# A planner's keys and DMA rates: attention into a gated FFN on one core, batch 0's v products and first half reordered

## The chip, the cores and the metric

The kernel runs on one core of one Trainium2 chip. The metric is the device time of one execution in microseconds: for the kernel before, the median of 8 runs is 378.05 us (376.56 to 378.98). The profile comes from one further execution, which took 377.98 us.

A core has five engines with queues of their own. TensorE (PE in the profile, PEld its weight loads) multiplies, VectorE (DVE), ScalarE (ACT) and GpSimd (POOL) compute, and SyncE (SP) here only issues DMA transfers. GpSimd issues DMA transfers as well, those that change the type on the way among them. Each queue is worked off in its order; between queues, semaphores make one wait for another.

## The reference

Inputs: q, k and v of shape (8, 8, 576, 64) (batch, heads, sequence, head width), s of shape (8, 8, 576), and the weights of the FFN, all float32.

```python
scores = scale * np.matmul(q, k.transpose(0, 1, 3, 2))
cum = np.cumsum(np.maximum(s, 0.0), axis=-1)
bias = -(cum[:, :, :, None] - cum[:, :, None, :])
scores = np.where(causal, -1e9, scores + np.minimum(bias, 0.0))
attn = softmax(scores);  out = np.matmul(attn, v)
x = out.transpose(0, 2, 1, 3).reshape(4608, 512)
xn = x / np.sqrt(np.mean(x * x, axis=-1, keepdims=True) + 1e-6) * rms_g
g = xn @ w_gate;  val = xn @ w_val          # 512 -> 1536
return (g * sigmoid(g) * val) @ w_out       # 1536 -> 512
```

Because cum rises along the sequence, the factor exp(-(cum_i - cum_j)) splits into a factor of the query, which the division by the sum cancels, and a factor exp(cum_j) of the key. The kernel multiplies v by that factor (the tiles vw, whose 65th column holds the factor itself, so that one matmul gives the sum as well).

## The kernel before, in words

**Order of the work.** The kernel first describes all of its operations to a planner (`Plan`, line 76), in Python, before anything runs. Each operation has an engine, a time in us that the planner counts for it, a `key` (lower goes first) and the operations that it depends on by the tiles that it reads and writes; `R.after(o, p)` (line 132) adds a dependence. `schedule` (line 136) then plays a list schedule: at each step it takes the engine that can start earliest, and on it, of the operations that are ready, the one with the lowest key; VectorE, ScalarE and GpSimd hold back for an operation of lower key that becomes ready within half of the candidate's time (line 199). What comes out is only the order on each engine; it is written into the program once, and on the chip each queue keeps it whatever the real times are. PSUM has 8 banks; each use names a group and how many banks the group may hold at once (`room`, line 162); `small_bank` (line 390) is a group of at most two.

**DMA transfers in the planner.** All transfers share one line: `dma_free` (line 148) is when the last one planned ends. A transfer begins at the later of that and its issue plus `lags[0]`, takes `dma`, and its data count as there `lags[1]` later (lines 216 to 219). Transfers that GpSimd issues go through 8 lanes (line 190). A transfer on SP may not be issued more than 3.0 us ahead of the end of all planned traffic (line 192). Rates stand in the helpers: `load_runs` (line 399, batches 0 and 1 of q and k in runs, cast to bf16 by GpSimd's transfers), `load_rows` (line 405, five blocks of 128 sequence positions, the last of 64), `load_w` (line 416, halves of the weights).

**Attention.** A batch has 4 head pairs and two halves, 8 units (`unit_scores`, line 539, `unit_av`, line 568). A unit's scores are three or five pairs of matmuls with K in place as weights, two exponentials on ScalarE into a tile E, and masks on GpSimd; Ea to Ed are the units of the first half (query blocks 0 and 1, of key blocks 0 and 1), Ee to Eh those of the second half, which also need key blocks 2 to 4. Then AV, on VectorE a reciprocal (rZ) and a product into x_blk. After a half's four units come its RMS norm (`attention`, line 628): squares summed (`att_square`, on ScalarE, for one block of batch 0 on VectorE), alpha = (mean + 1e-6)^-0.5 on GpSimd (`att_alpha`, tile al), and `att_out`: scale on ScalarE, four transposes on TensorE and a product with g into xnT, for batches 0 to 2. For batches 3 to 7 the scale is on VectorE and a DMA transpose on SP writes xnT. The keys are `key + step * (u + 1.5)` for a unit's AV and k2 = `key + step * 5.5` for the first half's norm; for batch 0 key is -78 and step 3, so that k2 is -61.5, which is the key of unit 4's AV too.

**K and Q.** Batches 0 and 1 come as runs (tiles raw, laid over q_nat and k_nat: batch 0 over q_nat, batch 1 over k_nat) and are transposed on TensorE (`prep_transpose`, line 427). For batches 2 to 7, SP loads fp32 rows into k_nat and q_nat, VectorE casts a block to bf16 (k_bf, q_bf) and a DMA transpose on SP writes the block into KT or QT (`prep_cast`, line 440). ScalarE squares all of K and Q for a check of magnitude (`raw_norm`, line 456, for batches 0 and 1). Of the tile k_nat, block i is free for batch 2 only once the i-th square of batch 1 is done. v has one tile (v_nat), whose block is free for the next batch when its product (`prep_v`, line 464; VectorE for batch 0, GpSimd after it) is done; the q and k loads of batch 2 wait for all of batch 1's products (line 766).

**FFN.** Nine chunks of 512 tokens (line 741). Chunk c has 12 or 24 pairs of matmul groups (`ffn1_group`), with tanh on ScalarE and two products on VectorE into Hs, then four output blocks (`ffn2`) whose stores go through SP. Keys of chunk c start at 36c. Attention of batch c+1 has keys from 36c + 1, its casts and transposes 36c - 14, the loads of batch c+2 36c + 16 in the order k, q, v, and the stores 36c. So on SP, in a chunk, stores go first when ready, then the transposes of the next batch, then the loads of the one after.

The setup of batch 0 begins at line 692. Its lines for v and attention, 723 to 731, are in the diff below; wl[2:], the second halves of the gate and value weights, wait for the mask of unit 3, and the runs of batch 1 for the first mask of unit 7.

Of the kernel before, what the change touches and what calls it, by code (L numbers as in the profile page):

```python
# [75 lines left out]
class Plan:  # L76
# [59 lines left out]
    def schedule(self):  # L136
        ops = self.ops
        for o in ops:
            o.succ = []
        left = {}  # L140
        for o in ops:
            left[o.n] = len(o.preds)
            for p in o.preds:
                ops[p].succ.append(o)
        free = {}
        table = {}
        pool = {}
        self.dma_free = 0.0
        order = []
        held = [[0.0, None] for _ in self.banks]  # L150

        def ready(o):
            t = 0.0
            for p, raw in o.preds.items():
                q = ops[p]
                if q.eng == o.eng and not q.dma:
                    t = max(t, q.done if raw and o.eng != "pe" else q.start)
                else:
                    t = max(t, q.done + self.HOP)
            return t  # L160

        def room(o):
            group, cap, n = o.takes[0].group, o.takes[0].cap, len(o.takes)
            for t in sorted(f for f, _ in held if f is not None):
                free = sum(1 for f, _ in held if f is not None and f <= t)
                busy = sum(1 for f, g in held if g == group and (f is None or f > t))
                if free >= n and busy + n <= cap:
                    return t
            return None

        lanes = [0.0] * self.LANES

        def add(o):
            pool.setdefault(o.eng, []).append((ready(o), o))

        for o in ops:
            if not left[o.n]:
                add(o)
        while any(pool.values()):
            best = None  # L180
            for e, cand in pool.items():
                f = free.get(e, 0.8)
                can = []
                for r, o in cand:
                    if o.takes:
                        t = room(o)
                        if t is None:
                            continue
                        r = max(r, t)
                    if o.dma and e == "pool":  # L190
                        r = max(r, lanes[0] + self.HOP)
                    if o.dma and e == "sp":
                        r = max(r, self.dma_free - 3.0)
                    can.append((o.key, o.n, r, o))
                if not can:
                    continue
                t = max(f, min(x[2] for x in can))
                k = min((x for x in can if x[2] <= t + 0.02), key=lambda x: x[:2])
                if e in ("dve", "act", "pool"):
                    soon = [x for x in can if x[:2] < k[:2] and x[2] < t + self.AHEAD * k[3].us]  # L200
                    if soon:
                        k = min(soon, key=lambda x: x[2])
                s = max(f, k[2])
                if best is None or s < best[0]:
                    best = (s, e, k[3], f)
            s, e, o, f = best
            pool[e] = [(r, q) for r, q in pool[e] if q is not o]
            o.wait = s - f
            if o.kind is not None:
                if table.get(e) not in (None, o.kind):  # L210
                    s += self.TABLE
                table[e] = o.kind
            o.start = s
            free[e] = s + o.us
            o.done = s + o.us + o.lat
            if o.dma:
                begin = max(self.dma_free, s + o.us + o.lags[0])
                self.dma_free = begin + o.dma
                o.done = self.dma_free + o.lags[1]
                if e == "pool":  # L220
                    lanes[:] = lanes[1:] + [o.done]
            for bank in o.takes:
                i = min((i for i, (t, _) in enumerate(held) if t is not None),
                        key=lambda i: held[i][0])
                bank.phys = i
                held[i][:] = [None, bank.group]
            for bank in o.uses:
                bank.left -= 1
                if not bank.left:
                    held[bank.phys][0] = max(u.done for u in bank.users) + self.HOP  # L230
            order.append(o)
            for q in o.succ:
                left[q.n] -= 1
                if not left[q.n]:
                    add(q)
        assert len(order) == len(ops)
        self.order = order
        return order
# [7 lines left out]
def kernel(  # L246
# [104 lines left out]
    def I(eng, method, us, key=None, kind=None, dma=0.0, lags=(1.2, 1.2), **kw):  # L351
        outs = [kw[n] for n in ("out", "accum_out") if n in kw]
        ins = [a for n, a in kw.items()
               if n not in ("out", "accum_out") and isinstance(a, (bass.AP, View))]
        f = getattr(ENG[eng], method)
        o = R.add(eng, us, lambda: f(**{n: real(a) for n, a in kw.items()}), outs, ins, key=key,  # L356
                  lat=LAT[eng], kind=kind, dma=dma,
                  name=outs[0].bank.name if isinstance(outs[0], View) else outs[0].name)
        o.lags = lags
        return o  # L360
# [37 lines left out]

    def load_runs(b, which, h0, h1, key):
        p0 = KP * which  # L400
        return I("pool", "dma_start", 0.8, key=key, dma=(4.0, 3.45)[b] * (h1 - h0) / 8, lags=(0.9, 1.3),
                 out=raw[b][p0 : p0 + KP, h0:h1, :, :].rearrange("p h c d -> p h (c d)"),
                 in_=(k, q)[which][b, h0:h1, :, :].rearrange("h (p c) d -> p h (c d)", c=KC))

    def load_rows(dst, src, b, eng, key):
        ops = []
        for sc in range(NB):
            n = 128 if sc < 4 else 64
            ops.append(I(eng, "dma_start", 0.88 if eng == "pool" else 0.4, key=key,
                         dma=1.28 * n / 128,  # L410
                         lags=(1.2, 1.2 if b < 2 else 4.2),
                         out=dst[0:n, sc], in_=src[b, :, sc * 128 : sc * 128 + n, :].rearrange(
                             "h p d -> p h d")))
        return ops

    def load_w(which, lo, hi, key):
        if which == 2:
            return I("pool", "dma_start", 0.84, key=key, dma=9.6 * (hi - lo) / 12,
                     out=wout_sb[:, lo:hi, :],
                     in_=moe_w_out[lo * 128 : hi * 128, :].rearrange("(fc p) d -> p fc d", p=128))  # L420
        dst, src = ((wg_sb, moe_w_gate), (wv_sb, moe_w_val))[which]
        return I("pool", "dma_start", 0.76, key=key, dma=8.9 * (hi - lo) / DF,
                 out=dst[:, :, lo:hi],
                 in_=src[:, lo:hi].rearrange("(cc p) f -> p cc f", p=128))

# [202 lines left out]
    def attention(b, key, step, cap):  # L628
        Es = {}
        two = 2 if b >= NTWO else 1  # L630
        sc = [unit_scores(b, range(u, u + two), [key + step * i for i in range(u, u + two)], Es,
                          max(cap, 2 * two)) for u in range(0, 2 * HP, two)]
        norms = []
        if b == 0:
            for u in range(HP + 1, 2 * HP):
                R.after(sc[u], sc[HP - 1])
        for hf in range(2):
            for u in range(HP * hf, HP * hf + HP):
                norms.append(unit_av(b, u, key + step * (u + 1.5), Es))
            tbs = (0, 1) if hf == 0 else (2, 3, 4)  # L640
            k2 = key + step * (HP * hf + HP + 1.5)
            for tb in tbs:
                att_square(b, tb, k2, "dve" if b == 0 and tb == 1 else "act")
            att_alpha(b, tbs[0], tbs[-1] + 1, k2)
            for tb in tbs:
                att_out(b, tb, k2)
        return norms
# [72 lines left out]
    for hp in range(HP):  # L720
        prep_transpose(0, 0, hp, -80 + hp, "dve")
        prep_transpose(0, 1, hp, -80 + hp, "act")
    gp_ = small_bank()
    mms(0.1, [(gp_[:, 0:CC], g4, ident_F[0:CC, 0:CC], True, True, True)], key=-75)
    I("dve", "tensor_copy", 0.1, key=-75, out=g_sb, in_=gp_[:, 0:CC])
    prep_w(0, "act", -70)
    vops = [prep_v(0, sc, "dve", -70) for sc in range(NB)]
    norms = attention(0, -78, 3, 4)
    R.after(vops[2], norms[2])
    for o in wl[2:]:  # L730
        R.after(o, masks[0, HP - 1])
    raw_norm(0, 20)
# [213 lines left out]
```

## Time and profile before

| what | value |
|---|---|
| median of 8 runs | 378.05 us (376.56 to 378.98) |
| profiled execution, its own time | 377.98 us |
| its span, first to last instruction | 376.2 us |
| instructions | 7766 |
| TensorE busy | 344.5 us, 92% |
| VectorE / ScalarE / GpSimd busy | 252.8 / 230.6 / 129.1 us |
| first FFN matmul | 27.02 us |
| granted clock at 0.5 | 192.05 to 195.46 us, and the end |
| chain that ended last | PE 56%, DVE 13%, DMA 11%, SP queue 6%, ACT 5% |
| first scores of batches 2 to 7 | 85.65, 117.14, 149.74, 189.83, 231.48, 272.38 us |

How to read it. The timeline lists an engine's instructions by start and duration, with the idle time ahead of them and what ended it in brackets; adjacent instructions of one kind are merged (x3). Tiles are named out<-in. SPq and POOLq are queues: an SP entry is the issue of a transfer, and what it waited for counts into its duration; when the data land is told by the trace's landing record. The table of waits adds up such idle times by the pair of waiting and releasing line. All helper operations carry line 356 and matmuls 371 or 373, so groups are told apart by their tiles. The granted clock is TensorE's, as a share of full speed.

### The profile page before, as it was taken

What the parts mean: (1) busy time and instruction counts of PE and PEld (TensorE: products, weight loads), DVE (VectorE), ACT (ScalarE), POOL (GpSimd) and SP (SyncE); (2) the same over time, 40 slices, a digit from 0 to 9 for tenths busy, and PEclk for the clock granted to TensorE, in tenths of its full rate; (3) what the DMA queues carried; (4) which work ended last, traced back from release to release, by engine and by line L of the source; (5) the groups of instructions that cost most, each with busy time, mean ns of one, the idle gap of its engine ahead of it and who ended that gap; (6) DMA issues with size and microseconds to landing.
All of it is one profiled execution on the core that took longest, in us unless ns stands there. A gap on an engine that the chain in (4) does not pass through costs nothing.

```text
span 376.2 us, 7766 instructions
## 1 busy us (share of the span) xinstructions
PE 344.5 (92%) x2907; PEld 208.7 (55%) x2934; DVE 252.8 (67%) x486; ACT 230.6 (61%) x469; POOL 129.1 (34%) x211
## 2 busy tenths in 40 slices
PE   3769999999999999799979988988999999999993
PEld 3548876698667874687425443444445444444441
DVE  6575954886946896489928893869578737816830
ACT  3857699697788827765657646871887533313321
POOL 8887334332561436133703470244323110000000
PEclk9999999999999999999989999999999999999998
DMA  7999994977996996689767986599650140011002
GB/s 121 212 225 208 198 178 102 192 172 151 187 167 173 172 190 127 180 155 197 133 107 183 194 169 115 146 201 193 114 153 9 30 129 19 0 73 42 0 34 86
DMA packets 138356, 51.13 MB, mean 136 GB/s; under 512 B 127300, under 2 KB 132936, under 8 KB 138312
## 3 DMA queue, kind: packets, MB, share of 16 engines
q1 hardware_dynamic: 131688, 41.13, 54.7%
q0 software_dynamic: 6624, 9.44, 14.3%
q8 instruction: 25, 0.41, 0.5%
q14 instruction: 19, 0.16, 0.2%
HBM read 38.16 MB, written 9.44 MB: 127 GB/s over the span
## 4 chain that ended last, share of the span: by engine, by line
PE 56%; DVE 13%; DMA 11%; SPq 6%; ACT 5%; issue 4%; POOL 3%; DVEq 0%; ACTq 0%; POOLq 0%
PE psc L373 8%; PE psh L373 7%; PE psb L373 7%; PE psg L373 7%; PE psd L373 7%; PE psa L373 7%; PE pse L373 6%; SPq L356 6%; PE psf L373 6%; DMA q_nat<-in_q_dram 4%; DVE Hs L356 3%; ACT sq_scr L356 3%; DMA v_nata<-in_v_dram 2%; DVE x_blkb L356 2%; DMA out_dram<-osbc 2%
## 5 line engine op out<-in xcount | busy, mean ns | idle before, releaser
L373 PEld LDWEIGHTS <-wv_sb 128*128 128x128 bf16 x624 | 60.9, 99 | 38.7 <-issue 6.3
L373 PEld LDWEIGHTS <-wg_sb 128*128 128x128 bf16 x624 | 59.1, 99 | 33.3 <-issue 5.5
L373 PEld LDWEIGHTS <-Hs 128*128 128x128 bf16 x432 | 41.3, 98 | 50.4 <-DVE Hs L356 2.7
L356 POOL TENSOR_TENSOR vwb<-v_nata,wT 128x512 bf16<-128x512 f32 (+1 forms) x20 | 21.1, 1071 | 13.4 <-DMA v_nata<-in_v_dram 13.0
L356 POOL TENSOR_SCALAR_AFFINE_SELECT Ea<-Ea 128x512 bf16<-128x512 bf16 x8 | 5.2, 647 | 59.1 <-ACT Ea L356 59.1
L356 ACT ACTIVATE sq_scr<-x_blka 128x512 bf16<-128x512 bf16 x19 | 12.0, 631 | 15.8 <-DVE x_blka L356 15.5
L373 PE MATMUL psf<-xnT,wv_sb 128*128 128x256 bf16 (+1 forms) x116 | 20.6, 313 | 0.2
L356 DVE CAST k_bf<-k_nat 128x512 bf16<-128x512 f32 (+1 forms) x30 | 17.1, 581 | 5.3 <-DMA k_nat<-in_k_dram 5.3
L356 ACT ACTIVATE sq_scr<-x_blkb 128x512 bf16<-128x512 bf16 x20 | 12.6, 630 | 12.5 <-DVE x_blkb L356 12.0
L356 POOL TENSOR_TENSOR vwa<-v_nata,wT 128x512 bf16<-128x512 f32 (+1 forms) x15 | 16.7, 1129 | 7.9 <-DMA v_nata<-in_v_dram 7.9
L356 DVE CAST q_bf<-q_nat 128x512 bf16<-128x512 f32 (+1 forms) x30 | 17.5, 593 | 2.8 <-DMA q_nat<-in_q_dram 2.8
L373 PE MATMUL pse<-xnT,wg_sb 128*128 128x256 bf16 (+1 forms) x102 | 18.2, 314 | 0.1
L373 PE MATMUL psd<-xnT,wg_sb 128*128 128x256 bf16 (+1 forms) x95 | 18.1, 325 | 0.1
L373 PE MATMUL psc<-wout_sb,Hs 128*128 128x512 bf16 x69 | 17.0, 379 | 1.1 <-DVE Hs L356 0.9
L373 PE MATMUL psh<-wout_sb,Hs 128*128 128x512 bf16 x70 | 16.6, 379 | 0.9 <-DVE Hs L356 0.8
L373 PE MATMUL psc<-xnT,wg_sb 128*128 128x256 bf16 (+1 forms) x83 | 15.2, 321 | 1.8 <-DVE xnT L356 1.3
L373 PE MATMUL psg<-wout_sb,Hs 128*128 128x512 bf16 x70 | 16.6, 379 | 0.1
L356 ACT ACTIVATE sq_scr<-q_bf 128x1024 bf16<-128x1024 bf16 (+1 forms) x18 | 16.5, 916 | 0.2
L373 PE MATMUL psb<-xnT,wg_sb 128*128 128x256 bf16 (+1 forms) x95 | 16.3, 307 | 0.1
L356 ACT ACTIVATE sq_scr<-k_bf 128x1024 bf16<-128x1024 bf16 (+1 forms) x18 | 16.3, 908 | 0.0
L373 PE MATMUL psb<-xnT,wv_sb 128*128 128x256 bf16 (+1 forms) x84 | 15.3, 322 | 0.2 <-DVE u_sbc L356 0.2
L356 DVE SCALAR_TENSOR_TENSOR x_blkb<-x_blkb,alb,gB 128x512 bf16<-128x512 bf16 x15 | 12.4, 876 | 4.6 <-POOL alb L356 4.5
(456 smaller groups left out, 859.2 us busy)
## 6 DMA issues: line engine op xcount, KB each, us to landing
k_nat<-in_k_dram SPq DMA_DIRECT2D x24, 256.0 KB, 4.7
q_nat<-in_q_dram SPq DMA_DIRECT2D x24, 256.0 KB, 5.4
v_nata<-in_v_dram SPq DMA_DIRECT2D x24, 256.0 KB, 5.0
out_dram<-osba SPq DMA_DIRECT2D x12, 256.0 KB, 2.3
out_dram<-osbb SPq DMA_DIRECT2D x12, 256.0 KB, 2.3
out_dram<-osbc SPq DMA_DIRECT2D x12, 256.0 KB, 2.4
v_nata<-in_v_dram POOLq DMA_DIRECT2D x8, 256.0 KB, 10.4
wg_sb<-in_moe_w_gate_dram POOLq DMA_DIRECT2D x2, 768.0 KB, 12.2
```

Source lines behind the costliest of these rows:

```text
L356: o = R.add(eng, us, lambda: f(**{n: real(a) for n, a in kw.items()}), outs, ins, key=key, lat=LAT[eng], kind=kind, dma=dma, name=outs[0]. ...
L373: nc.tensor.matmul(out, lhsT=lhsT, rhs=rhs, start=st, stop=sp)
```

## The change

Seven places change; the set of operations and their data stay the same.

- In the planner, an SP transfer may be issued from 2.0 us ahead of the end of the last transfer of SP's own queue (`sp_free`), no longer 3.0 us ahead of the end of all traffic. The single line of traffic, dma_free, stays for when a transfer begins.
- The counted DMA times of `load_runs`, `load_rows` and `load_w` become smaller.
- The key k2 of batch 0's first half goes from -61.5 to -64.5; unit 5's mask has key -63, unit 6's -60, unit 7's -57.
- The transpose of g takes a bank of a group of its own.
- The v products of batch 0 keep the key -70 for key blocks 0 and 1 and get -62 for blocks 2 to 4; block 2's product is made to follow the normalisation of unit 3 (before: of unit 2), whose AV has the key -64.5.

```diff
         lanes = [0.0] * self.LANES
+        sp_free = 0.0
...
                     if o.dma and e == "sp":
-                        r = max(r, self.dma_free - 3.0)
+                        r = max(r, sp_free - 2.0)
...
                 o.done = self.dma_free + o.lags[1]
+                if e == "sp":
+                    sp_free = self.dma_free
...
-        return I("pool", "dma_start", 0.8, key=key, dma=(4.0, 3.45)[b] * (h1 - h0) / 8, lags=(0.9, 1.3),
+        return I("pool", "dma_start", 0.8, key=key, dma=(3.95, 3.35)[b] * (h1 - h0) / 8, lags=(0.9, 1.3),
...
-                         dma=1.28 * n / 128,
+                         dma=(1.08 if eng == "pool" else 1.2) * n / 128,
...
-            return I("pool", "dma_start", 0.84, key=key, dma=9.6 * (hi - lo) / 12,
+            return I("pool", "dma_start", 0.84, key=key, dma=8.0 * (hi - lo) / 12,
...
-        return I("pool", "dma_start", 0.76, key=key, dma=8.9 * (hi - lo) / DF,
+        return I("pool", "dma_start", 0.76, key=key, dma=7.8 * (hi - lo) / DF,
...
-            k2 = key + step * (HP * hf + HP + 1.5)
+            k2 = key + step * (HP * hf + HP + 1.5) - (3 if b == 0 and hf == 0 else 0)
...
-    gp_ = small_bank()
+    gp_ = bank("g", 1)
     mms(0.1, [(gp_[:, 0:CC], g4, ident_F[0:CC, 0:CC], True, True, True)], key=-75)
     I("dve", "tensor_copy", 0.1, key=-75, out=g_sb, in_=gp_[:, 0:CC])
     prep_w(0, "act", -70)
-    vops = [prep_v(0, sc, "dve", -70) for sc in range(NB)]
+    vops = [prep_v(0, sc, "dve", -70 if sc < 2 else -62) for sc in range(NB)]
     norms = attention(0, -78, 3, 4)
-    R.after(vops[2], norms[2])
+    R.after(vops[2], norms[3])
```

## The prediction

> **What bounds the kernel now.** First the page, for the shares of the engines: TensorE is busy 92% of the span, every other engine under 70%. The table by windows then says where TensorE is not busy: 11.1 us of the first 27.02 us, 1.5 us from there to 120 us, 12.8 us between 120 and 282 us, 6 us after that. So there are two places to win: the start, and the middle. The last 94 us hold TensorE work alone.
>
> The start, from the timeline (start, duration, engine, line, operation):
> ```profile
> 18.13 1.28 DVE L356 TENSOR_TENSOR vwa<-v_nata,psc 128x512 bf16<-128x512 f32 x2 [0.40 <-DMA v_nata<-in_v_dram]
> ...
> 19.87 0.68 DVE L356 TENSOR_TENSOR vwa<-v_nata,psc 128x512 bf16<-128x512 f32 x1
> 20.47 0.42 DVE L356 TENSOR_TENSOR x_blka<-psb,rZd 128x256 bf16<-128x256 f32 x1
> ...
> 20.92 0.94 DVE L356 SCALAR_TENSOR_TENSOR sq_scr<-x_blka 128x512 bf16<-128x512 bf16 x1
> ...
> 21.97 0.62 POOL L356 TENSOR_SCALAR_AFFINE_SELECT Eh<-Eh 128x512 bf16<-128x512 bf16 x1
> ...
> 22.69 0.19 POOL L356 TENSOR_SCALAR ala<-ssa 128x2 f32<-128x2 f32 x1
> ...
> 23.73 1.33 ACT L356 ACTIVATE x_blka<-x_blka,ala 128x512 bf16<-128x512 bf16 x2 [2.08 <-POOL ala L356]
> ```
> Three v products (vwa) stand in front of the last normalisation of the first half, and a mask of the second half (Eh) stands in front of alpha. That row of waits ends in the first FFN matmul at 27.02 us.
>
> The middle, from the waits of TensorE and from the timeline of the SP queue alone (waits: total, times, longest):
> ```profile
> PE psf L373 <- DMA QTb<-q_bf: 2.4, 1, 2.4
> PE psb L373 <- DMA QTa<-q_bf: 1.6, 1, 1.6
> ...
> PE psf L373 <- DMA QTa<-q_bf: 0.9, 1, 0.9
> ```
> ```profile
> 47.21 2.68 SPq L356 DMA_DIRECT2D k_nat<-in_k_dram  x2
> 49.94 3.16 SPq L356 DMA_DIRECT2D q_nat<-in_q_dram  x2
> 59.19 2.60 SPq L356 DMA_DIRECT2D k_nat<-in_k_dram  x3
> 61.88 3.94 SPq L356 DMA_DIRECT2D q_nat<-in_q_dram  x3
> 65.93 5.36 SPq L356 DMA_DIRECT2D v_nata<-in_v_dram  x5
> 71.38 1.32 SPq L356 DMA_TRANSPOSE KTa<-k_bf  x1
> ```
> The same view goes on without a gap to 282.2 us: each entry starts where the one before ends. The loads of batches 3 to 7 begin at 88.28, 123.29, 162.27, 202.62 and 242.44 us, so a round takes 39 to 40 us once the x transposes are in it, of which the 15 loads take 16.9 us (162.27 to 179.17). TensorE waits in batches 4, 5 and 6 for the third block of Q that comes out of this row; after the 2.4 us wait the granted clock is 0.5 for 3.4 us, which costs another 1.7. So from 59 us on **the SP queue is what the middle hangs on**, and it starts late: it stands idle from 53.1 to 59.19 us for k blocks 2 to 4, whose buffer ScalarE's squares of batch 1's raw keys release at 59.17, 60.35 and 61.10 us. Three q and five v loads are queued behind them.
>
> **The change, part by part.** No instruction is added or removed; the planner only orders the same ones anew.
>
> *The g bank.* The transpose of g leaves the group of small banks. In the trace it held one from 9.68 to 10.22 us, and the Q transposes of the last heads wait for their data, landed at 11.72 us. That landing hides it: 0. Without that cover it would give the 0.5 us of the bank, and take as much if another bank were short.
>
> *v products, earlier key of the first half.* The products of blocks 2 to 4 cost 1.28 + 0.68 = 1.96 us of VectorE. The AV of pairs 2 and 3 end at 18.35 and 18.93 us; two reciprocals and two products (0.17 + 0.42 + 0.14 + 0.42) after that could end at 19.6 instead of 20.89: 1.3 us. VectorE is idle from 17.72 us, so the planner may still put one product there, which waits for its load until 18.10: 0.9 us. I take 1.0. The square (0.94 + 0.08) then ends at 20.9, ScalarE's (behind the exponentials that end at 20.6) at 21.4, alpha starts at 21.4 in place of 22.69 if the mask stands behind it: 1.3 us, and the FFN could start at 25.7 us.
>
> What is late next: the second half. Its first AV needs the three products, now after the square: 20.9 + 2.0 = 22.9 us instead of 20.61. From there TensorE has four AVs of 0.65 us and two transposes of 0.61 us, 3.8 us, to do: 26.7 us. So TensorE gets 0.3 us of the 1.3 (1.0 if one product went early). In return it is busy without a break from 22.9 us. Before, its full clock came at 31.62 us, 4.6 us after the FFN began; until then the first three groups of 8 matmuls took 1.87, 1.71 and 1.44 us instead of 0.87, 2.4 us too much. Up to 2 us of this can go. I take 1.5 us for the start; the ends are a loss of 0.5 (the products still later) and a gain of 3.3 (1.3 + 2.0).
>
> [...]
>
> *Rates of the pool's DMAs.* Landings in the trace come every 3.7 us for half a weight (21.97 to 35.03 us, less two v loads of 1.0, over three); the planner had 4.45, now 3.9. v loads 1.02 and 0.99 us (1.28, now 1.08); runs of batch 1 1.66 (1.73, now 1.68); the first half of w_out 3.14 (4.8, now 4.0). Added up in the planner, the pool's traffic ended at 57 us and now ends at 51; the trace has 52.55. The q runs of batch 1 were due at 45.3, now 41.6; landed 41.68. TensorE reaches their transposes at 43.33 us, so the earlier place costs nothing; without that cover a wait of up to 1 us.
>
> *The SP rule.* Until now no SP transfer was issued before 3 us short of the end of all traffic, the pool's included: not before 54 us in the planner, by when k blocks 2 to 4 were nearly free, which is why they stand ahead of the rest. Now the first k load is free to go when the v products of batch 1 are done (46.4 us); it counts itself behind the 51 us of the pool, so the second goes at about 50.2 and the rest every 1.2 us. At 51.4 to 55 us k blocks 2 to 4 are still not free, and what is free takes their place: q blocks 0 to 4, and after them v. On the chip the 6.1 us of idle queue are then filled with q loads. With the release at 61.1 us unmoved, five v loads remain after the last k (5.4 us): the transposes start at 67.3 instead of 71.38, **4.1 us earlier**. With the release earlier by the 1.5 us of the start it is 5.6; with one q load (0.6 us) left over, 5.0. Ends: 0 (order unchanged) and 7 (v before k too). I take 4.8, near the two middle rows.
>
> Moved past: the pool's w_out loads. The second took 4.2 us beside two SP loads against 3.14 for the first. Beside six, an estimate from these rows is 2 us later than 52.55; the first use is at 60.6 us, so it is hidden, and costs what is over 6 us.
>
> *Middle rounds.* 13.5 full loads at 1.28 less 3.0 us of lead, or at 1.2 less 2.0: 14.3 and 14.2 us. The two edits cancel, and the planner's rounds stay as they are. Both are short of the trace (16.9 us), so the queue goes on falling behind as before. The first scores of batches 4 to 6 stand directly behind the first FFN group of their chunk, where their keys put them, so I expect them at the same place.
>
> **The sum.** TensorE arrives 1.5 us earlier; the queue's data 4.8 us earlier. Waits of 1.6, 2.4 + 1.7 and 0.9 us (6.6) can shrink by what the queue gains on TensorE; when the first two are gone, TensorE runs into the queue again in batch 5 or 6, so the end moves with the queue: 4.8 us, of 1.5 + 6.6 at most. The profiled execution took 377.98 us, 1.8 over its span of 376.2 and 0.07 under the median of 378.05; 378.05 - 4.8 = 373.3, for which I say 373.5, as a new order can add a small wait.
>
> **Rivals.**
> *The queue keeps its start.* If the planner's squares of the raw keys move forward as well, k stays ahead of q and v, and the gain of the start is given back at the third block of Q: 378.05 less at most 0.9, about 377.4. For it: ScalarE is 99% busy from 48 to 60 us, so the squares move by little; against it: that also keeps k late. 17%.
> *More than the queue.* v before k, 7 us, and all waits gone: 369 to 371. 9%.
> *Slower.* Fewer microseconds of lead make the queue reach the end of a load block with the casts not done, and loads of the next batch go ahead of the third Q block. Three k loads cost 2.6 us (the row at 59.19), and a wait of that length brings 1.7 of slow clock: 4.3 us in a batch, two batches 8.6. It decides where it exceeds the 4.8 of lead; net 380 to 382. For it: a planner that counts 14.2 us for 16.9. Against: the transposes have the lower keys. 18%.
> The forecast, 371 to 376.9: 56%.
>
> What a measurement here can tell from no change is 0.3%, 1.1 us. Faster by more: 56 + 9 = 65%; within: 17%; slower: 18%. The range leaves out 6% below and 13% above: 370 to 379.6. The start alone, from a loss of 0.5 to a gain of 3.3, and the queue's 0 to 7 lie inside it.
>
> **What would show it.** Right: alpha of batch 0 before 21.8 us, first FFN matmul between 25.5 and 26.8; on SP q blocks ahead of k block 2, first K transpose at 65.5 to 67.5 us, last SP transpose at 277 to 278; the Q waits of batches 4 to 6 shorter. Wrong: an SP queue still idle from 53 to 59 us, or new TensorE waits of over 1 us at places where there were none.

## The result, and the profile after

The changed kernel takes 375.17 us (median of 22 runs, 372.29 to 377.22); the kernel before, run beside it, 377.95. The ratio is 0.993, with a 95% interval of 0.9911 to 0.9948: **0.7% faster, 2.8 us of the 4.6 us that were forecast**. The profiled execution has a span of 374.0 us, 2.2 less than before.

The start comes first, in the timeline of the kernel after (start, duration, engine, line, operation; the helper that was line 356 is now 359, matmuls are 374 and 376):
```profile
18.39 1.29 DVE L359 TENSOR_TENSOR vwa<-v_nata,psc 128x512 bf16<-128x512 f32 x2 [0.53 <-DMA v_nata<-in_v_dram]
...
20.36 0.42 DVE L359 TENSOR_TENSOR x_blka<-psg,rZd 128x256 bf16<-128x256 f32 x1
...
20.81 0.69 DVE L359 SCALAR_TENSOR_TENSOR sq_scr<-x_blka 128x512 bf16<-128x512 bf16 x1
...
21.43 0.69 DVE L359 TENSOR_TENSOR vwa<-v_nata,psc 128x512 bf16<-128x512 f32 x1
21.70 0.19 POOL L359 TENSOR_SCALAR ala<-ssa 128x2 f32<-128x2 f32 x1 [0.83 <-ACT sq_scr L359]
22.17 0.43 PE L376 MATMUL psd<-vwa,Ee 128*128 128x65 bf16 x5 [2.40 <-DVE vwa L359]
...
25.87 1.90 PE L376 MATMUL psc<-xnT,wg_sb 128*128 128x256 bf16 x8
```
Only the third v product went behind the square of the first half; two still fill VectorE's gap at 18.39 us. alpha comes at 21.70 us (22.69 before), the first FFN matmul at 25.87 (27.02). TensorE pays for the late third product with a wait of 2.40 us ahead of the second half's AV. Its clock record shows full speed from 28.30 us; before, it was 31.62.

Then the SP queue alone, whose entries from 47.21 to 71.38 us were shown for the kernel before:
```profile
32.04 2.33 SPq L359 DMA_DIRECT2D v_nata<-in_v_dram  x2
44.34 0.37 SPq L359 DMA_DIRECT2D k_nat<-in_k_dram  x1
44.76 8.80 SPq L359 DMA_DIRECT2D q_nat<-in_q_dram  x2
55.01 3.78 SPq L359 DMA_DIRECT2D k_nat<-in_k_dram  x4
58.84 3.60 SPq L359 DMA_DIRECT2D q_nat<-in_q_dram  x3
62.55 3.54 SPq L359 DMA_DIRECT2D v_nata<-in_v_dram  x3
66.19 1.35 SPq L359 DMA_TRANSPOSE KTa<-k_bf  x1
```
The first K transpose comes 5.2 us earlier. Of the idle stretch from 53.1 to 59.19 us, 1.45 us are left (53.56 to 55.01); but no more q loads than before went ahead of k blocks 2 to 4: two, as at 49.94 us in the kernel before, and the second of them, begun at 48.09 us, held the queue for 5.47 us. What moved the queue are two other things. Two v loads went out at 32.04 us, so three are left where five were: the row behind the last k is 7.2 us long (58.84 to 66.1) instead of 9.4. And the squares released the last k block at 58.11 us, 3.0 earlier than before. In batch 7 the lead is 3.9 us: the last K or Q transpose ends at 278.3 us; before, it was 282.2. From there to the end are 95.7 us, before 94.0.

Last, the waits of TensorE after 27 us (total, times, longest):
```profile
PE pse L376 <- DVE u_sbc L359: 2.7, 1, 2.7
PE psc L376 <- DVE u_sbc L359: 1.6, 1, 1.6
PE psh L376 <- DMA QTb<-q_bf: 1.6, 1, 1.6
PE psh L376 <- DMA QTa<-q_bf: 1.5, 1, 1.5
PE psd L376 <- DVE u_sbc L359: 1.2, 1, 1.2
PE psd L376 <- ACT osba L359: 1.1, 1, 1.1
```
The waits for Q shrank from 4.9 us (2.4 + 1.6 + 0.9) to 3.1, but did not go (that of batch 6 grew from 0.9 to 1.5), and FFN products (u_sbc) and output buffers (osba) came in their place. All idle times of TensorE over 0.15 us behind its first FFN matmul add up to 13.1 us, before to 12.9. The windows say where TensorE stands idle (length, then busy time and count of each engine, TensorE first); the first line is the middle before, the others are after:
```profile
120.00:282.00 162.00, 149.20 (x1179) 86.11 (x1192) 119.96 (x226) 105.78 (x225) 61.20 (x93) 0.99 0.84 159
```
```profile
27.02:120.00 92.98, 91.56 (x1014) 69.54 (x1017) 66.98 (x133) 79.41 (x164) 40.49 (x65) 1.00 0.96 182
120.00:282.00 162.00, 149.16 (x1174) 86.43 (x1188) 114.93 (x225) 104.41 (x218) 60.55 (x92) 0.98 0.83 157
```
12.84 us of the middle are idle; before it was 12.80. The largest of these waits is read on VectorE, in the kernel after and then at the same place before:
```profile
248.85 0.58 DVE L359 CAST q_bf<-q_nat 128x512 bf16<-128x512 f32 x1 [1.60 <-DMA q_nat<-in_q_dram]
249.97 0.43 DVE L359 CAST q_bf<-q_nat 128x512 bf16<-128x512 f32 x1 [0.54 <-DMA q_nat<-in_q_dram]
250.32 0.68 DVE L359 SCALAR_TENSOR_TENSOR u_sbc<-T_sbc,pse 128x512 bf16<-128x512 f32 x1
```
```profile
252.98 0.56 DVE L356 CAST q_bf<-q_nat 128x512 bf16<-128x512 f32 x1 [1.61 <-DMA q_nat<-in_q_dram]
253.46 0.67 DVE L356 SCALAR_TENSOR_TENSOR u_sbc<-T_sbc,pse 128x512 bf16<-128x512 f32 x1
```
Two casts of Q stand ahead of the FFN's product in VectorE's order and wait for their loads. Before, it was one cast, and TensorE, at the end of that row, lost 1.75 us with no change of the clock. Now it loses 2.71 us, and the granted clock is 0.5 from 250.17 for 6.83 us:
```profile
251.05 1.87 PE L376 MATMUL pse<-xnT,wv_sb 128*128 128x512 bf16 x4 [2.71 <-DVE u_sbc L359]
252.71 1.91 PE L376 MATMUL psf<-xnT,wg_sb 128*128 128x512 bf16 x4
```
These groups follow each other at 1.7 us instead of 0.87. Added up: FFN start 1.15 us; half clock at its begin 2.43 instead of 4.60 us (ahead of the clock record's first entry; in after, the groups of 8 there start 1.69 and 1.24 us apart, from 28.80 us on 0.87), worth 1.1; gaps minus 0.2; slow clock in the middle 6.83 instead of 3.41 us, minus 1.7. These are estimates, and they make only 0.35 of the 2.2 us by which the spans differ. The rest lies in a shorter busy time of TensorE (342.9 us by the page, before 344.5), and its cause was not found.

### The profile page after: what moved, and what is told of

It reads as the page before. It is cut to its first block, busy times and chain, and to the rows that moved or that the text cites. A ratio compares the mean times of both kernels' runs of the same rounds, so it can differ in the third digit from the quotient of the medians.

```text
span 374.0 us, 7756 instructions
## 1 busy us (share of the span) xinstructions
PE 342.9 (92%) x2907; PEld 208.4 (56%) x2934; DVE 248.7 (66%) x486; ACT 231.6 (62%) x469; POOL 129.9 (35%) x211
## 4 chain that ended last, share of the span: by engine, by line
PE 65%; DMA 11%; DVE 7%; SPq 4%; ACT 4%; POOL 4%; issue 3%; ACTq 0%; DVEq 0%; POOLq 0%
PE psd L376 9%; PE psa L376 8%; PE psf L376 8%; PE psc L376 8%; PE pse L376 8%; PE psh L376 8%; PE psg L376 8%; PE psb L376 7%; SPq L359 4%; DMA k_nat<-in_k_dram 4%; DMA v_nata<-in_v_dram 3%; DMA q_nat<-in_q_dram 2%; DMA out_dram<-osbb 1%; POOL vwa L359 1%; DVE u_sbc L359 1%
## 5 line engine op out<-in xcount | busy, mean ns | idle before, releaser
L359 DVE CAST k_bf<-k_nat 128x512 bf16<-128x512 f32 (+1 forms) x30 | 17.1, 578 | 6.8 <-DMA k_nat<-in_k_dram 6.8
L359 ACT ACTIVATE sq_scr<-x_blka 128x512 bf16<-128x512 bf16 x19 | 12.0, 629 | 11.6 <-DVE x_blka L359 11.2
L376 PE MATMUL pse<-xnT,wv_sb 128*128 128x256 bf16 (+1 forms) x83 | 15.2, 319 | 2.8 <-DVE u_sbc L359 2.7
L376 PE MATMUL psh<-xnT,wv_sb 128*128 128x256 bf16 (+1 forms) x95 | 17.5, 316 | 0.2
L376 PE MATMUL psg<-xnT,wg_sb 128*128 128x256 bf16 (+1 forms) x100 | 17.6, 311 | 0.1
L359 DVE CAST q_bf<-q_nat 128x512 bf16<-128x512 f32 (+1 forms) x30 | 15.9, 534 | 2.1 <-DMA q_nat<-in_q_dram 2.1
L376 PE MATMUL psd<-wout_sb,Hs 128*128 128x512 bf16 x69 | 16.5, 379 | 0.6 <-DVE Hs L359 0.4
L376 PE MATMUL psd<-xnT,wv_sb 128*128 128x256 bf16 (+1 forms) x72 | 14.3, 334 | 2.3 <-DVE u_sbc L359 1.2
L376 PE MATMUL psa<-xnT,wg_sb 128*128 128x256 bf16 (+1 forms) x90 | 16.3, 314 | 0.1
L376 PE MATMUL psc<-wout_sb,Hs 128*128 128x512 bf16 x69 | 16.2, 379 | 0.2
L376 PE MATMUL psc<-xnT,wv_sb 128*128 128x256 bf16 (+1 forms) x84 | 14.4, 308 | 1.6 <-DVE u_sbc L359 1.6
L376 PE MATMUL psf<-xnT,wg_sb 128*128 128x256 bf16 (+1 forms) x80 | 15.3, 328 | 0.1
## 6 DMA issues: line engine op xcount, KB each, us to landing
wg_sb<-in_moe_w_gate_dram POOLq DMA_DIRECT2D x2, 768.0 KB, 12.4
```

Source lines behind the costliest of these rows:

```text
L376: nc.tensor.matmul(out, lhsT=lhsT, rhs=rhs, start=st, stop=sp)
```

## Experiments

Theory A is the one behind the forecast: the end moves with the time at which the SP queue starts on batch 2. Rival B: the end moves with the start of the FFN. Theory C, formed after the first four runs: the time follows how near the planned block of 15 loads is to the 16.9 us that the chip takes. C2, formed after the next four: the longer the planner's SP round, the more FFN work its order puts ahead of the first scores, which hang on late data, and the waits for Q go. D: the gain is in the SP rule as such, whatever the lead. E: each new order deals the waits anew, without a pattern. F: the gain with rows of 1.28 was one lucky order. "Rows" are `load_rows` of SP. Each was timed in five rounds beside the kernel before (377.18, 377.55 and 378.06 us in three groups of four). The ratio with its interval is an estimate of its own, up to 0.3% away from the quotient of the two medians; differences between runs of different groups are no finer than that.

The planned load block that is used below follows from the code: a load's data begin at the earliest 0.4 + 1.2 us behind its issue, so 15 loads (13.5 full ones) and the lead to the next issue make 1.6 + 13.5 x rows - lead. On the chip, in the kernels before and after, the block takes 16.9 to 17.1 us in most rounds where nothing else stands in it, and 18.3 to 18.5 us in the others.

**Before with the keys alone.**
```diff
-            k2 = key + step * (HP * hf + HP + 1.5)
+            k2 = key + step * (HP * hf + HP + 1.5) - (3 if b == 0 and hf == 0 else 0)
...
-    gp_ = small_bank()
+    gp_ = bank("g", 1)
...
-    vops = [prep_v(0, sc, "dve", -70) for sc in range(NB)]
+    vops = [prep_v(0, sc, "dve", -70 if sc < 2 else -62) for sc in range(NB)]
...
-    R.after(vops[2], norms[2])
+    R.after(vops[2], norms[3])
```


> Keys of batch 0 and the g bank alone; planner's rates and SP rule as before. Theory A (the SP queue's early loads make the gain): first FFN matmul at 25.5 to 26.5 us, SP queue still idle for several us before k blocks 2 to 4, first K transpose of batch 2 not before 69 us, time 377 to 378, at most 1 us under before. Rival B (the gain is the start of batch 0): 375 to 376, as the whole change.


Measured: 377.18 us, ratio 0.9994 (0.9968 to 1.002). The start gains all that was hoped: FFN at 24.83 us, full clock at 26.79. And nothing of it is left at the end, as the waits of TensorE behind 27 us show:
```profile
PE psa L373 <- DMA QTa<-q_bf: 5.9, 3, 2.9
PE pse L373 <- DMA QTb<-q_bf: 2.4, 1, 2.4
PE psf L373 <- DMA QTb<-q_bf: 1.6, 1, 1.6
```
Waits for Q of 2.94, 2.38, 2.73 and 1.58 us in batches 4 to 7 take it back; three of them are followed by 3.41 us of granted clock 0.5. B falls. The SP queue moves too, more than A allowed (not before 69 us): the last k block is free at 58.2 us, as in after, and the first K transpose comes 3.2 us earlier than before.
```profile
68.14 1.31 SPq L356 DMA_TRANSPOSE KTa<-k_bf  x1
```

**Before with the SP rule alone.**
```diff
-                        r = max(r, self.dma_free - 3.0)
+                        r = max(r, sp_free - 2.0)
```
(and the lines that keep `sp_free`, as in the change)


> The SP rule alone (own queue, 2.0 us), old rates and keys. A: two v loads of batch 2 go out before 40 us, first K transpose 2 to 4 us under 71.4, time 375 to 376.5. B: first FFN matmul at 27 us as before, time 378.


Measured: 369.27 us, 0.9768 (0.9737 to 0.98), far below every expectation. The queue hardly leads: two v loads go out at 31.84 us, but all five k loads stand ahead of the q loads. Its first K transpose comes at 70.32 us (before 71.38),
```profile
70.32 1.33 SPq L359 DMA_TRANSPOSE KTa<-k_bf  x1
```
and its last K or Q transpose ends at 278.8 (282.2). One wait for Q is left,
```profile
PE psc L376 <- DMA QTb<-q_bf: 1.8, 1, 1.8
```
and all gaps are 6.5 us against 12.9.

**Before with the new rates alone.**
```diff
-        return I("pool", "dma_start", 0.8, key=key, dma=(4.0, 3.45)[b] * (h1 - h0) / 8, lags=(0.9, 1.3),
+        return I("pool", "dma_start", 0.8, key=key, dma=(3.95, 3.35)[b] * (h1 - h0) / 8, lags=(0.9, 1.3),
...
-                         dma=1.28 * n / 128,
+                         dma=(1.08 if eng == "pool" else 1.2) * n / 128,
```
(and `load_w` as in the change)


> The new rates alone, old SP rule (3.0 us ahead of all traffic) and old keys. A: the planner's pool traffic ends 6 us earlier, so two v loads go ahead and q blocks pass k blocks as in the whole change; first K transpose 4 us under 71.4, time 375 to 376.5. B: 378.


Measured: 380.15 us, 1.0046 (1.0019 to 1.0073): slower. Yet its SP queue is far ahead: first K transpose 66.77 us, and the last K or Q transpose ends at 270.1 us, 12 us ahead of before and the earliest of the first four experiments. **A falls here**: the end stands 109 us behind that, not 94. The waits of TensorE have moved from Q to the output buffers:
```profile
PE psf L373 <- ACT osbb L356: 3.7, 1, 3.7
PE psd L373 <- ACT osba L356: 3.5, 1, 3.5
PE pse L373 <- ACT osbc L356: 2.4, 1, 2.4
```
There are three of them for the four output blocks of a chunk, and the fourth copy waits for the first's store. ScalarE's timeline has the first copy and the fourth,
```profile
186.08 0.58 ACT L356 ACTIVATE osba<-pse 128x512 f32<-128x512 f32 x1
...
197.04 0.60 ACT L356 ACTIVATE osba<-psd 128x512 f32<-128x512 f32 x1 [5.12 <-DMA out_dram<-osba]
```
and SP's timeline shows why the store, ready at 186.7 us, was not issued until 193.55:
```profile
186.51 1.20 SPq L356 DMA_TRANSPOSE KTb<-k_bf  x1
187.82 1.21 SPq L356 DMA_TRANSPOSE QTb<-q_bf  x1
189.48 2.06 SPq L356 DMA_TRANSPOSE KTb<-k_bf  x1
191.64 1.19 SPq L356 DMA_TRANSPOSE QTb<-q_bf  x1
192.88 0.58 SPq L356 DMA_DIRECT2D k_nat<-in_k_dram  x1
193.55 0.53 SPq L356 DMA_DIRECT2D out_dram<-osba  x1
```
The queue keeps the planned order, and in it this store stands behind four transposes and a load, at a place that the real queue reaches late.

**SP rule and rates, no keys.** (the two edits above together)


> SP rule and rates, without the keys of batch 0 and without the g bank. A: all of the queue's head start, first FFN matmul at 27 us, time 375 to 376. B: 378.


Measured: 374.98 us, 0.9921 (0.9891 to 0.9952), the time of the full change. So in the full change the keys are worth nothing at the end, and the rates take 5.7 us (374.98 - 369.27) from what the SP rule alone gains.

**After, with the old rate of SP's rows.**
```diff
-                         dma=(1.08 if eng == "pool" else 1.2) * n / 128,
+                         dma=(1.08 if eng == "pool" else 1.28) * n / 128,
```


> The changed kernel with SP's rows counted at 1.28 us again (pool rows stay at 1.08). Planned load block of 13.5 full rows: 1.6 + 17.3 - 2.0 = 16.9 us, as in the trace (16.9); the changed kernel has 15.8. Theory C (the time follows how near the planned load block is to the chip's 16.9 us): 369 to 372. Rival D (the queue's early start decides; it is the same as in the changed kernel): 374 to 376. Rival E (each new order deals the waits anew, without a pattern): anywhere in 369 to 380.


Measured: 368.04 us, 0.9775 (0.9745 to 0.9805). One number in the planner undone gives 6 us by the ratios, 7 by the medians. This is for C, and against D: the block goes from 15.8 to 16.9 us. The SP queue itself is scarcely different: first K transpose 65.98 us (after: 66.19), rounds of 38.5, 34.7, 40.0, 39.6 and 39.4 us (38.4, 34.8, 39.2, 41.9, 39.9).

**Before, with a shorter lead in the old rule.**
```diff
-                        r = max(r, self.dma_free - 3.0)
+                        r = max(r, self.dma_free - 2.4)
```


> The kernel before with one number changed: SP transfers up to 2.4 us ahead of the end of all traffic, no longer 3.0. Planned load block 1.6 + 17.3 - 2.4 = 16.5 us, pool traffic still holding SP back at the start. C: 370 to 373. D: no early v or q loads, 377.


Measured: 375.61 us, 0.9964 (0.9933 to 0.9996). The sign is C's, the size is not. 9 groups of FFN matmuls now stand ahead of the first scores of batches 3 and 4 (8 and 2 before), but 2.8 ahead of batches 5 to 7, and waits for Q add up to 12.3 us.

**Before, with SP's own queue and the old lead.**
```diff
-                        r = max(r, self.dma_free - 3.0)
+                        r = max(r, sp_free - 3.0)
```
(and the lines that keep `sp_free`)


> The kernel before with the SP rule on its own queue, but the lead left at 3.0 us: planned load block 15.9 us as before, with the early v loads of batch 2. C: 376 to 378. D: 369 to 372, as with the SP rule at 2.0 us.


Measured: 378.95 us, 1.0064 (1.0036 to 1.0092), with 10.2 us of waits for Q. That is above what either expected. D falls: the same rule gives 369.27 with a lead of 2.0 us and loses with 3.0.

**After, with a lead of 0.9 us.**
```diff
-                        r = max(r, sp_free - 2.0)
+                        r = max(r, sp_free - 0.9)
```


> The changed kernel with its rates (rows 1.2 us) and a lead of 0.9 us: planned load block 1.6 + 16.2 - 0.9 = 16.9 us by another way than in the run with rows at 1.28. C: 369 to 372. D: 374 to 376.


Measured: 428.26 us, 1.1343 (1.13 to 1.1386). C's number was wrong because the edit does more than lengthen the block: below 1.6 us of lead, the planner leaves a hole behind each transfer. Its transposes stand 1.52 us apart instead of 1.27 and its stores 1.42 instead of 0.4, which makes a planned round of some 45 us. SP's real rounds became 45 to 51 us, and the first scores of batches 2 to 7 come behind all 24 FFN groups of the chunk, so that little or no FFN work is left beside the attention: TensorE's gaps are 40.9 us, the most of them for masks of GpSimd and for xnT, and the granted clock is 0.5 for up to 17.07 us at a time. Not a test of the block alone, but it shows that a planned round can be too long.

**After, with rows of 1.34 and of 1.42.** Here the block is lengthened by its rate alone.
```diff
-                         dma=(1.08 if eng == "pool" else 1.2) * n / 128,
+                         dma=(1.08 if eng == "pool" else 1.34) * n / 128,
```


> The changed kernel with SP rows at 1.34 us, lead 2.0: planned load block 17.7 us, planned round (15 transposes of 1.27 and 4 stores of 0.4 added) 38.4; the chip's rounds are 39 to 40. Theory C2 (the planner puts the first scores of a batch later, behind more FFN groups of the chunk, the longer its SP round is, and TensorE then no longer waits for Q): 366 to 369, first scores of batches 4 to 7 behind 10 groups or more. Rival F (the gain of the run with rows at 1.28 was one lucky order): 370 to 378.

> SP rows at 1.42 us: planned load block 18.8, planned round 39.4, as long as the chip's. C2: 366 to 370 and no wait for Q over 1 us; if the planner counts SP longer than TensorE's chunk, attention drifts late and the time rises (a lead of 0.9 us did that with a planned round of 45 us: 428). F: no relation to the run with 1.34.


Measured: 362.94 us (360.84 to 366.43), 0.9594 (0.954 to 0.9648), and 360.56 us (359.18 to 361.8), 0.9526 (0.9485 to 0.9568). **The second beats both kernels, by 4.7% the one before.** C falls, as the block moves away from 16.9 us and the time still sinks; F falls; C2 has the direction and the places of the scores (11 groups or more from batch 4 on), but both times lie below its ranges. The longest waits of the second by TensorE after 27 us are
```profile
PE psc L376 <- DVE u_sba L359: 0.6, 1, 0.6
PE psg L374 <- DVE Hs L359: 0.4, 1, 0.4
```
None is for Q or an output buffer; all gaps are 2.7 us, and the clock stays at 1.0 from 28.37 us to 359.5. Against after, gaps shrink by 10.4 us and 6.83 us of half clock go, worth 3.4 by the same estimate as above: 13.8 of the 13.9 us between the spans. In the windows, the middle has 2.81 us of idle TensorE in place of 12.84:
```profile
120.00:282.00 162.00, 159.19 (x1253) 92.96 (x1267) 131.44 (x241) 111.10 (x231) 65.96 (x94) 1.00 0.87 159
```
Its SP queue is no faster than after's: rounds of 35.7 to 39.7 us, last K or Q transpose 276.5 (278.3). Its order is another too, with two x transposes among the v loads, but that does not bring Q sooner: the third Q block of batch 5 lands at 194.04 us, in after at 188.46. What removes the wait is TensorE's order. Batch 5's first scores, in the timeline of TensorE of the kernel after and then of this one:
```profile
185.66 1.03 PE L376 MATMUL psb<-xnT,wv_sb 128*128 128x512 bf16 x4
186.62 0.28 PE L376 MATMUL psh<-QTb,KTb 64*128 64x256 bf16 x1
...
188.50 0.27 PE L376 MATMUL psh<-QTb,KTb 64*128 64x256 bf16 x1 [1.59 <-DMA QTb<-q_bf]
...
191.10 1.02 PE L376 MATMUL psd<-xnT,wv_sb 128*128 128x512 bf16 x4 [1.13 <-ACT osba L359]
```
```profile
194.87 1.03 PE L376 MATMUL pse<-xnT,wv_sb 128*128 128x512 bf16 x4
195.74 1.03 PE L376 MATMUL psa<-xnT,wg_sb 128*128 128x512 bf16 x4
196.69 0.28 PE L376 MATMUL psd<-QTb,KTb 64*128 64x256 bf16 x1
...
197.24 0.82 PE L376 MATMUL psc<-xnT,wv_sb 128*128 128x512 bf16 x3
```
In after, they follow the first pair of FFN groups and meet data that aren't there; in this one they follow 16.8 groups (the last two of an unbroken row are shown), come 2.65 us behind the landing, and run through.

**After without the keys, rows of 1.28.** (SP rule and rates, with 1.28 for SP's rows)


> As the changed kernel with SP rows at 1.28, but with the keys of batch 0 and the g bank as before. If the queue no longer takes it away, the start's 1 to 1.5 us show now: 369 to 370, that is 1 to 2 us above the same with the keys (368.0). If the start is worth nothing: 368.


Measured: 372.67 us, 0.9864 (0.9813 to 0.9915). With the keys it was 368.04: here they go with 3.4 us by the ratios, 4.6 by the medians, more than either expectation had, where at rows of 1.2 they went with nothing.

**Before, with rows of 1.356 on SP under the old rule.** The block is 16.9 us, as with the SP rule alone.
```diff
-                         dma=1.28 * n / 128,
+                         dma=(1.28 if eng == "pool" else 1.356) * n / 128,
```


> The kernel before, with the old SP rule (3.0 us ahead of all traffic), and SP rows counted at 1.356 us: planned load block 1.6 + 18.3 - 3.0 = 16.9 us by a third way, nothing else changed. C2: first scores of batches 4 to 7 behind more than 2 groups, 369 to 373. Rival D (the queue's own rule is needed): 377.


Measured: 376.63 us, 0.9963 (0.9931 to 0.9995). The time is D's. Under the old rule a longer block alone does not place the scores late, though C2 expected it: 7.8 groups stand ahead of the first scores of batch 5, but 2 and 1.8 in batches 6 and 7, and waits for Q are 10.8 us.

All together, by planned block; "groups" are FFN groups of matmuls (24, or 12 pairs, in every chunk) that TensorE runs in a chunk before the first scores of batches 4 and 7, a fraction where a matmul has no record or lies elsewhere; gaps are those of TensorE over 0.15 us behind its first FFN matmul, and 0 for Q is less than 0.4 us; the times are medians, each beside its own runs of the kernel before:

| version | rule, lead, rows | block, us | groups, batch 4 / 7 | gaps, us | of it Q | time, us |
|---|---|---|---|---|---|---|
| rates alone | all, 3.0, 1.2 | 14.8 | 2 / 1.8 | 15.3 | 0 | 380.15 |
| after | own, 2.0, 1.2 | 15.8 | 2 / 1.8 | 13.1 | 3.1 | 375.17 |
| before | all, 3.0, 1.28 | 15.9 | 2 / 1.8 | 12.9 | 4.9 | 377.95 |
| SP rule and rates | own, 2.0, 1.2 | 15.8 | 2 / 1.8 | 11.2 | 0 | 374.98 |
| keys alone | all, 3.0, 1.28 | 15.9 | 2 / 1.8 | 12.4 | 9.9 | 377.18 |
| own queue, old lead | own, 3.0, 1.28 | 15.9 | 2 / 1.8 | 13.4 | 10.2 | 378.95 |
| shorter lead | all, 2.4, 1.28 | 16.5 | 9 / 2.8 | 14.3 | 12.3 | 375.61 |
| old rule, 1.356 | all, 3.0, 1.356 | 16.9 | 4 / 1.8 | 14.1 | 10.8 | 376.63 |
| after without keys, 1.28 | own, 2.0, 1.28 | 16.9 | 2 / 3.8 | 10.8 | 7.5 | 372.67 |
| SP rule alone | own, 2.0, 1.28 | 16.9 | 12 / 13.8 | 6.5 | 1.8 | 369.27 |
| after, 1.28 | own, 2.0, 1.28 | 16.9 | 2 / 10.8 | 8.9 | 6.0 | 368.04 |
| after, 1.34 | own, 2.0, 1.34 | 17.7 | 11 / 15.8 | 3.3 | 0 | 362.94 |
| after, 1.42 | own, 2.0, 1.42 | 18.8 | 14 / 21.8 | 2.7 | 0 | 360.56 |

With 15 transposes of 1.27 us and four stores of 0.4 the planned round of the last row is 39.4 us (18.8 + 19.05 + 1.6), inside the 38.4 to 41.9 us that most of the chip's rounds take; after's is 36.4. Four rows with a block of 16.9 us take from 368.04 to 376.63 us, so the block alone does not set the time. The groups ahead of batch 7 follow it better: the five rows with more than 3 are the five fastest, and the two with the most lead.

## Why the prediction was right or wrong

- *Start.* Right in its signs: alpha below 21.8 us, FFN at 25.87 in the range of 25.5 to 26.8, full clock earlier. What was called late next, the second half's AV, is the new 2.40 us wait. The FFN started 1.15 us earlier and 2.17 us of half clock went, worth 1.1: 2.2 us where 1.5 were taken. The full clock came at 28.30 us, 2.43 us behind the first FFN matmul (before: 31.62, 4.60 behind). As a term of the end it is nothing at rows of 1.2 (374.98 without the keys, 375.17 with them) and nothing alone (0.9994).
- *g bank, rates of the pool.* No wait at either place was found. They were not run apart from each other.
- *SP rule, start of the queue.* Right in the number, 66.19 us against 65.5 to 67.5, and by luck: the way there was another. The prediction had q blocks 0 to 4 fill the idle stretch while the release of k hardly moved, with five v loads left. In the trace two q blocks went ahead, as before; the release came 3.0 us earlier (1.5 were counted at most), and two v loads had gone out at 32.04 us, 2.2 us of row, which was not foreseen. Nor is it the SP rule that does it: alone it moves the first K transpose by 1.1 us, the keys alone by 3.2, the rates alone by 4.6. The last transpose at 278.3 is 0.3 late.
- *Middle rounds.* "The two edits cancel, and the planner's rounds stay as they are" holds, 15.9 to 15.8 us, and the scores of batches 4 to 6 stayed where they were, behind two groups (those of batches 2 and 3 moved forward, from 15 and 8 groups to 11 and 4). But this was read as harmless. Apart, the SP rule gives minus 2.3% and the rates plus 0.5%: the lower rate for SP's rows gave back most of what the shorter lead brings.
- *The sum: the step that failed in size.* "The end moves with the queue: 4.8 us." The queue gained 5.2 us at its start and 3.9 at its end; the kernel 2.8. The sum counted the waits for Q alone. In the new order TensorE's waits for u_sbc and output buffers grew from 2.9 to 7.5 us, against 1.8 us less for Q, and the slow clock in the middle doubled. The rates alone show that the step fails as a rule too: 12 us of queue, and no gain. That 375.17 lies inside the range says little for the sum, as the range reached from 371 to 376.9.
- *Signs.* One of the signs of being wrong came: new waits of over 1 us where there were none, for u_sbc at 122 and 161 us (1.22 and 1.60) and for osba at 190 us (1.13). And of the signs of being right one came in part: the wait for Q went in batch 4 and shrank in batch 5, but grew in batch 6.
- *Rivals.* "The queue keeps its start" did not come: the first transpose is 5.2 us earlier. "Slower" named loads ahead of the third Q block; in after they stand behind the Q blocks of their round, as at 198.53 us. "More than the queue" did not come in this version, but a change of one number (1.28, 1.34, 1.42) brings it, by another way than the one named: v before k was not needed.

**What is shown and what stays open.** Shown: with SP's own queue and a lead of 2.0, raising SP's counted rate from 1.2 over 1.28 and 1.34 to 1.42, and nothing else, takes 14.6 us away step by step, while the real queue's rounds start within 3 us of after's (238.1 against 238.4 us in the last), and TensorE's gaps go with it. That the placing of scores does it is argued from the traces: Q lands later in the fastest version, and nothing waits for it. No run moved the scores alone by their keys. Open: why the old rule with a block of 16.9 us (376.63) moves them in the first batches only; why the keys are worth 3.4 to 4.6 us at 1.28 and nothing at 1.2, and why the run without keys and with the old rates of the pool (369.27) beats the one with the new (372.67), since each edit deals the whole order anew; and whether more than 1.42 gains more. With 2.7 us of gaps left there, waits have little more to give.

## What to carry to other kernels

A list schedule is as good as the length that it counts for a queue's whole round, not only for one transfer: compare the planned round with the trace's and bring it up to that. Here a planned round of 36.4 us was 15 us slower at the end than one of 39.4, and one of 45 us, reached by a lead of 0.9, another 53 us slower. A rate that is too low did not slow the queue down here; it put consumers directly at data that were not there, and an edit that makes the queue earlier is then lost in the next wait. Two edits that cancel in such a sum should be run apart, since one of them may be worth three times the two together, as the SP rule was (minus 2.3% alone, minus 0.8% with the rates).

## What the runs showed of the hardware

- In these traces, the run with a lead of 0.9 left aside, TensorE has 22 gaps of 1.85 us and more behind its first FFN matmul. With 16 of them the granted clock fell to 0.5, during the gap or up to 1.5 us behind it: 13 times for 3.41 us, as with 1.85 us (SP rule alone) and 2.43 (before), and three times for 6.83 us, with 2.71 (after), 3.28 and 3.55 (old rule, 1.356). With six it did not fall: 1.97 and 3.10 (after with 1.28), 1.98 and 2.40 (shorter lead), 2.62 (SP rule and rates) and 3.49 (rates alone). No gap under 1.85 us, such as 1.75 (before), was followed by a fall. So the same gap may cost nothing, or, by an estimate from groups at 1.7 us instead of 0.87, 1.7 or 3.4 us more.
- Two transfers that SP issued while GpSimd's own were under way came late: in after, the v loads issued at 32.04 and 34.00 us landed at 45.81 and 52.59, 13.8 and 18.6 us later; the median of the page is 5.2 us for v. The second q issue of the row at 44.76 us held the queue for 5.47 us, with no wait named in the trace.
- In after, an issue of a DMA transpose holds the SP queue for 1.22 us (median), and the next mostly starts 1.31 us after it, so the 15 of a round take longer (19.6 us, an estimate from these numbers) than the 15 loads (16.9 us).
